# Sparse attention and a routed MLP on one core: the first five attention units in another order, one batch's values by way of DRAM, two weights loaded later

## The chip, the cores and the metric

One NeuronCore of a Trainium2 chip runs the whole program. TensorE (PE) multiplies, VectorE (DVE), ScalarE (ACT) and GpSimd (POOL) do element-wise work, and DMAs are issued from the queues of SyncE (SP), ACT and POOL. Each engine takes its instructions in the order in which the program gives them, and waits at the first one whose operands or buffers are not ready. Times are microseconds (us) on the device. The time of a kernel is the median of its runs.

## What is computed

The reference, cut to what matters (8 batches, 8 heads, 512 local and 32 global tokens, heads of 64; 8 experts, model width 512, hidden width 1024):

```python
def attention(q_l, k_l, v_l, q_g, k_g, v_g):
    scale = 1 / sqrt(64)
    v_all = concatenate([v_g, v_l], axis=2)
    # the 32 global queries see every key
    s_g = scale * q_g @ concatenate([k_g, k_l], axis=2).T
    out_g = softmax(s_g) @ v_all
    # a local query sees the global keys and the local keys at most 32 positions away
    s_ll = where(abs(i - j) <= 32, scale * q_l @ k_l.T, -1e9)
    s_l = concatenate([scale * q_l @ k_g.T, s_ll], axis=-1)
    out_l = softmax(s_l) @ v_all
    return concatenate([out_g, out_l], axis=2)

def routed_mlp(x, w_gate, w1, w2):            # x: the 4352 tokens of the attention, 512 wide
    P = exp(x @ w_gate - max)
    for _ in range(8):                        # rows, then columns, are brought to a fixed sum
        P /= P.sum(1, keepdims=True) + 1e-9
        P /= P.sum(0, keepdims=True) + 1e-9
        P *= N / E
    for e in range(8):
        out += P[:, e:e+1] * (maximum(x @ w1[e], 0) @ w2[e])
```

Inputs and the output are 32-bit floats. The kernel works in 16-bit floats with sums in 32 bits.

## The kernel before

**Units.** The local attention is cut into 32 units. Unit n is a pair of heads, hp = n mod 4, of batch n // 4. Eight blocks of 64 queries of each of the two heads lie side by side, and a block sees 128 local keys and the 32 global ones. The steps of a unit are functions, and each gives work to several engines:

- `st_A(n)`: eight transposes on PE bring the unit's keys and queries into the tile "pt". DVE copies the keys to `kTe[n % 8]`, ACT the queries to `qbd[n % 2]` (two copies).
- `st_B0(n, part)` for batch 0, `st_B(n, part)` for the others, parts 0, 1 and 2 with three, three and two blocks: the scores on PE. In batch 0 the mask is added by PE with the matrix `m16`, DVE takes the minima (the scores have their sign turned), and ACT takes the exponentials. From batch 1 on one DVE instruction adds `mask` and takes the minima, and the exponentials read its output. Batch 0 reads the global keys from `kg0T`, the others from `kgT`.
- `st_N(n, ...)`: DVE divides the exponentials by their sums in two pieces, and POOL divides the columns of the global keys ("Pl").
- `st_D1(n)`: eight transposes of the divided exponentials on PE, one copy on DVE ("pw"). `st_D2(n)`: two transposes of Pl on PE, one copy on ACT ("pg").
- `st_E(n)`: 32 matmuls with the values, and one copy of the result into `xT[batch]` (on ACT in batch 0, on DVE in batch 1). With the last unit of a batch SP stores `xT` to DRAM (`xd`).

**Values.** `st_E` needs the values of a batch in rows of 128 tokens in two alignments: `va` begins 32 tokens ahead of the first one, `vb` 32 tokens behind it. Batches 0 and 1 load them with four consecutive tokens in each partition (`load_vrow`), POOL casts them to the one tile `vsr` in two halves (`cast_vrow`), and `select_v` picks the rows for block j of `va` or `vb` by four matmuls with the 0/1 matrix `zsel` into a PSUM tile "pv", which DVE (even j) or ACT (odd j) copies. The later batches load both alignments from DRAM (`load_v`).

**Buffers.** Tiles with one tag take turns in a fixed number of buffers. PSUM has two buffers for "tr" (pt, the D1 and D2 transposes, the transposes of the global keys), two for "sc" (scores of parts 0 and 1), two for "mm" (scores of part 2 in batch 0, pv, the hidden layer's ph) and one for "po" (the result of E, one pv in each select_v that names it, and the global queries' scores). An instruction that fills a buffer waits for the last reader of what was in it.

**Global queries.** `cast_g` on POOL casts the global keys and queries, `transpose_g` on PE brings them to `kgT` and `qgT`, and `st_G0` to `st_G3` compute their attention in between.

**Hidden layer in the gaps.** From slot 4 on `f1(...)` puts single tiles of the hidden layer x @ w1[e] of experts 0 to 3 between the attention's steps: four matmuls of 512 columns on PE into "ph", then ACT ("a") or DVE ("v") takes the maximum with zero into `hT`. `f1("aa")` is two of them. They need all four heads' pairs of the batch in `xT`, and the weights `w1e[e]`, which POOL loads with a cast (`load_w1e`, 1 MB each, on POOL's DMA queue). What the attention did not take is done in the iterations over P and behind them (`tail_run`). Then the rest of the experts runs.

**Order.** Nothing reorders the program: the order of the calls is the order on each engine and in each DMA queue. Units 0 to 3 are the loop `for s in range(HP)` from L518 on: scores of unit s, D1 and D2 of unit s-1, loads and casts that depend on s, A of unit s+1, selections, divisions of unit s; E of units 0 to 2 comes in where selections allow it. From unit 4 on, the loop `for s in range(HP, NU + 1)` has a pass for each slot s: scores of unit s in three parts, D1, D2 and E of unit s-1, A of unit s+1, f1 between them, divisions at the end. The pass of slot 4 has a branch of its own, with most of batch 1's selections and the two ACT-queue copies that fill the rest of `vb` from `va`.

The helper `tt` (L672) issues most DVE operations of the second half. In the profile L346 is the division, L334 the minima, L338 and L309 the exponentials, L155 the selections, L466 the hidden layer's matmuls, L378 and L381 E.

Of the kernel before, what the change touches and what calls it, by code (L numbers as in the profile page):

```python
# [23 lines left out]
def kernel(  # L24
# [19 lines left out]
    P = 128  # L44
# [45 lines left out]
    with tc.tile_pool(name="att_c", bufs=1) as att_c, \  # L90
# [21 lines left out]
        vg16 = [dscr.tile([Sg, H, Dh], FP16, name=f"vg16_{b}") for b in range(B)]  # L112

# [29 lines left out]
        def cast_vrow(b):  # L143
            f = vraw.pop(b)
            for g in range(2):
                h = slice(4 * g, 4 * g + 4)
                nc.gpsimd.tensor_copy(out=vsr[:, :, h, :], in_=f[:, h].rearrange("p h s d -> p s h d"))

        def select_v(b, t, js, po=()):
            for j in js:  # L150
                c0 = P * j + HB * t
                pool, tag = (ps_po, "po") if j in po else (ps_mm, "mm")
                pv = pool.tile([P, D], FP32, tag=tag, name="pv")
                for so in range(NJ):
                    nc.tensor.matmul(pv, zsel[:, so, c0 : c0 + P], vsr[:, so], start=(so == 0), stop=(so == NJ - 1))  # L155
                cp = nc.vector.tensor_copy if j % 2 == 0 else nc.scalar.copy
                cp(out=vab[b % 2][t][:, j], in_=pv.rearrange("p (h d) -> p h d", h=H))

# [82 lines left out]
        nc.gpsimd.memset(m16[:, 2, 3 * W : KW], HUGE)  # L241
        init_vgz(vgz[0], nc.gpsimd)
# [275 lines left out]
        for s in range(HP):  # L518
            for part in range(3):
                st_B0(s, part)  # L520
            if s == 3:
                st_E(1)
            if s >= 1:
                st_D1(s - 1)
                st_D2(s - 1)
            if s == 0:
                cast_vrow(0)
                cast_qk(0, 1, gq)
                load_qk(1, 0, (nc.sync, nc.sync))
                load_g(k_g, kgf)  # L530
                load_w1e(0)
                nc.vector.memset(qbd[1], 0.0)
            elif s == 1:
                load_vrow(1)
                load_qk(1, 1, (nc.sync, nc.sync))
                load_vg(1)
                init_vgz(vgz[1], nc.gpsimd)
                load_vz(1)
                qgf = hpool.tile([P, H, NJ * Dh], FP32, tag="hT", name="qgf")
                load_g(q_g, qgf)  # L540
            elif s == 2:
                load_w1e(1)
                nc.gpsimd.dma_start(out=wg_sb, in_=moe_w_gate.rearrange("(dko dki) e -> dki dko e", dki=P))
                cast_qk(1, 0, gq)
                gk0 = cast_g(kgf, 0)
            for t in (kTe[s + 2],) if s < 3 else kTe[5:7]:
                nc.vector.memset(t[:, 0:W], 0.0)
                nc.vector.memset(t[:, W + Sl :], 0.0)
            st_A(s + 1)
            if s < 2:  # L550
                select_v(0, s, (0, 1), (0,))
            st_N(s, 0, 6)
            if s == 0:
                select_v(0, 0, (2, 3), (3,))
            elif s == 2:
                select_v(0, 1, (2, 3))
                st_E(0)
            st_N(s, 6, NHB)
            if s == 3:
                st_E(2)  # L560
            if s == 2:
                cast_vrow(1)
            if s == 3:
                transpose_g(gk0, 0, kgT)
                for t in qgbd:
                    nc.vector.memset(t, 0.0)
                select_v(1, 0, range(2))
                load_w1e(2)
                nc.vector.memset(mask[:, :, KW:SW], 0.0)
                nc.scalar.mul(mask[:, :, 0:KW], m16, -HUGE * 8.0)  # L570
        gat = {s: s - 5 for s in range(5, 9)}
        gat.update({2 * j + 1: j for j in range(4, NU // 2)})
        for s in range(HP, NU + 1):
# [8 lines left out]
            if s == HP:  # L582
                st_B(s, 0)
                st_D1(s - 1)
                st_D2(s - 1)
                select_v(1, 0, range(2, NJ))
                st_E(s - 1)
                select_v(1, 1, (NJ - 1,))
                slot = s + 1
                va, vb = vab[1]  # L590
                nc.scalar.dma_start(out=vb[0:HB, 0 : NJ - 1], in_=va[HB:P, 0 : NJ - 1])
                nc.scalar.dma_start(out=vb[HB:P, 0 : NJ - 1], in_=va[0:HB, 1:NJ])
                cast_qk(1, 1, gq)
            else:
                if s <= 2 * HP:
                    st_B(s, 0)
                st_D1(s - 1)
                if g23:
                    st_GN(*gp)
# [9 lines left out]
            if s < NU:  # L609
                st_B(s, 1)  # L610
            if s > HP:
                f1("va")
            if s + 1 < NU:
                st_A(s + 1)
            if s < NU:
                st_B(s, 2)
            f1("v")
            if s > HP:
                st_E(s - 1)
# [8 lines left out]
            if s < NU:  # L628
                st_N(s, 0, 6)
                st_N(s, 6, NHB)  # L630
            if s == HP:
                gcast = [(cast_g(x[0], x[1]), x) for x in ((kgf, 1, kgT), (qgf, 0, qgT), (qgf, 1, qgT))]
                load_w1e(3)
# [377 lines left out]
```

## Time and profile before

| | us |
|---|---|
| median of 3 runs | 1057.38 (1055.8 to 1061.52) |
| profiled execution | 1057.3 |
| its span, first to last instruction | 1055.5 |
| PE busy | 1025.4 |
| DVE busy | 809.6 |
| ACT busy | 489.4 |
| POOL busy | 132.2 |

"Busy" is the time in which an engine carries out instructions. Line 2 of the profile cuts the span into 40 slices of 26.4 us and gives the busy share of each in tenths; PEclk is the clock that PE was granted, as a share of its full one. Units 0 to 3 lie in the first 38 us, and unit 5's pass ends at about 61 us. A line in order of time begins with the start and the duration and ends with the idle time of the engine ahead of it and what ended that. A window's line gives each engine's busy time in it.

Some marks of the time before: the first scores of units 0 to 6 start on PE at 8.0, 14.4, 20.5, 27.4, 37.9, 47.8 and 61.3 us (of unit 6 its first part after the pass of slot 5). E(4) starts at 56.2. The weights w1e(0) to w1e(3) are issued at 13.4, 21.8, 35.2 and 52.7, the four loads of batch 2's queries and keys between 48.7 and 51.3.

### The profile page before, as it was taken

To read this page: it belongs to the slowest core of one execution; us is meant where nothing else is said; L and a number is where in the kernel's file an instruction comes from. 1 tells how busy PE (TensorE), PEld (TensorE's weight loads), DVE (VectorE), ACT (ScalarE), POOL (GpSimd) and SP (SyncE) were. 2 spreads that over 40 slices of the span, in tenths; PEclk is the share of its full clock that TensorE was granted. 3 is DMA by queue.
4 is the path that set the end of the run, shared out by engine and by line. 5 is a ranking of instruction groups with operands and counts; after the bars stand their busy time and mean duration, and the time that the engine had idled before them with its cause. 6 is when DMAs were issued, how large, how long until landed. Compare 5 with 4: busy or idle time off the path is not lost.

```text
span 1055.5 us, 21693 instructions
## 1 busy us (share of the span) xinstructions
PE 1025.4 (97%) x8854; PEld 700.0 (66%) x8854; DVE 809.6 (77%) x1466; ACT 489.4 (46%) x1248; POOL 132.2 (13%) x215
## 2 busy tenths in 40 slices
PE   7799999999999999999999999999999999999998
PEld 4455555555554466677777777777777777777787
DVE  8587777777776776997877877778777787688685
ACT  7678888787886674222222223223223233132231
POOL 7441423413313002000000000000000000000000
PEclk9899999999999999999999999999999999999999
DMA  9887598987945999935435435335336435535441
GB/s 273 200 193 211 106 261 203 218 239 156 255 130 170 270 275 303 259 106 189 170 112 194 154 140 195 125 141 199 143 117 200 168 117 177 209 100 184 170 165 31
DMA packets 97348, 190.82 MB, mean 181 GB/s; under 512 B 33425, under 2 KB 63585, under 8 KB 84449
## 3 DMA queue, kind: packets, MB, share of 16 engines
q1 hardware_dynamic: 54208, 159.61, 43.6%
q0 software_dynamic: 40432, 20.20, 14.8%
q10 hardware_dynamic: 2608, 9.64, 2.4%
q8 instruction: 69, 1.13, 0.4%
q14 instruction: 31, 0.25, 0.1%
HBM read 157.11 MB, written 53.62 MB: 200 GB/s over the span
## 4 chain that ended last, share of the span: by engine, by line
PE 79%; DVE 9%; ACT 7%; issue 3%; DMA 1%; POOL 0%; ACTq 0%; SPq 0%; DVEq 0%; POOLq 0%
PE m L795 26%; PE ph L752 21%; PE ph L466 15%; PE pm L795 10%; ACT Pu L309 3%; DVE Pu L346 3%; PE ptw L357 1%; DVE h L672 1%; ACT hT L469 1%; PE pt L273 1%; ACT qbd L283 1%; DMA h<-hd 1%; PE po L378 1%; PE sc L299 1%; DVE m L409 1%
## 5 line engine op out<-in xcount | busy, mean ns | idle before, releaser
L754 ACT ACTIVATE h<-ph 128x512 f16<-128x512 f32 (+1 forms) x288 | 164.8, 573 | 405.9 <-PE ph L752 397.1
L752 PE MATMUL ph<-xs,w1s 128*128 128x512 f16 (+1 forms) x1152 | 269.4, 367 | 2.0 <-DVE o L811 2.0
L466 PE MATMUL ph<-xT,w1e 128*128 128x512 f16 (+1 forms) x1152 | 257.2, 368 | 0.2
L795 PEld LDWEIGHTS <-h 128*128 128x128 f16 x2144 | 209.8, 98 | 44.1
L795 PE MATMUL m<-w2c,s 128*128 128x256 f16 x1620 | 199.9, 273 | 0.0
L672 DVE TENSOR_TENSOR s<-h 128x1024 f16<-128x1024 f16 (+2 forms) x140 | 122.8, 919 | 91.2 <-ACT h L754 46.8
L795 PEld LDWEIGHTS <-s 128*128 128x128 f16 x1620 | 158.5, 98 | 38.2
L466 PEld LDWEIGHTS <-w1e 128*128 128x128 f16 x1152 | 105.6, 98 | 96.6 <-issue 4.5
L752 PEld LDWEIGHTS <-w1s 128*128 128x128 f16 x1152 | 112.7, 98 | 84.8 <-issue 2.3
L672 DVE TENSOR_TENSOR h<-h,pb 128x4096 f16<-128x4096 f16 (+1 forms) x35 | 148.3, 4237 | 3.1 <-DMA h<-hd 2.9
L795 PE MATMUL m<-w2c,h 128*128 128x256 f16 x1072 | 134.2, 273 | 0.0
L469 ACT ACTIVATE hT<-ph 128x512 f16<-128x512 f32 (+1 forms) x191 | 103.8, 558 | 47.5 <-PE ph L466 46.1
L795 PE MATMUL pm<-w2c,h 128*128 128x256 f16 x1072 | 122.9, 273 | 0.0
L672 DVE TENSOR_TENSOR xs<-xg,pb 128x2048 f16<-128x2048 f16 (+1 forms) x36 | 78.0, 2168 | 46.1 <-DMA pb<-pd 40.9
L309 ACT ACTIVATE Pu<-ms,mx 128x160 f16<-128x160 f32 x224 | 93.6, 420 | 3.9 <-DVE mx L306 1.5
L471 DVE TENSOR_SCALAR hT<-ph 128x512 f16<-128x512 f32 x97 | 66.8, 689 | 31.3 <-PE ph L466 30.6
L672 DVE TENSOR_TENSOR h<-h 128x1024 f16<-128x1024 f16 (+1 forms) x140 | 86.8, 661 | 0.0
L306 DVE CUSTOM_DVE_ANT_0 ms<-sc,mask 128x160 f32<-128x160 f32 x224 | 59.9, 320 | 24.5 <-PE sc L301 22.0
L350 POOL TENSOR_TENSOR Pl<-Pu,rs 128x256 f16<-128x256 f16 x32 | 24.7, 771 | 196.7 <-DVE rs L345 131.6
L811 DVE SCALAR_TENSOR_TENSOR o<-m,o 128x512 f32<-128x512 f32 (+1 forms) x72 | 43.3, 655 | 5.2 <-ACT o L809 3.5
L346 DVE TENSOR_TENSOR Pu<-Pu,rs 128x768 f16<-128x768 f16 x64 | 45.1, 705 | 2.2
L309 ACT ACTIVATION_READ_ACCUMULATOR Pu<-ms,mx 128x1 f32 x224 | 42.4, 189 | 0.0
(157 smaller groups left out, 903.7 us busy)
## 6 DMA issues: line engine op xcount, KB each, us to landing
w1s<-w1d SPq DMA_DIRECT2D x36, 1024.0 KB
h<-hd SPq DMA_DIRECT2D x32, 1024.0 KB
hd<-hT SPq DMA_DIRECT2D x26, 1024.0 KB
pb<-pd SPq DMA_DIRECT2D x64, 256.0 KB
w2c<-in_moe_w_dram POOLq DMA_DIRECT2D x16, 512.0 KB, 21.0
out_dram<-o SPq DMA_DIRECT2D x8, 1024.0 KB
f<-in_q_l_dram SPq DMA_DIRECT2D x15, 512.0 KB
f<-in_k_l_dram SPq DMA_DIRECT2D x15, 512.0 KB
```

What stands on the lines that cost most here:

```text
L306: nc.vector.tensor_tensor_reduce(out=ms[:, ii, :], in0=sc[:, SW * ii : SW * (ii + 1)], in1=mask[:, mi, :], scale=-scale, scalar=BIG, op0=A ...
L309: nc.scalar.activation(out=d["Pu"][:, i, :], in_=ms[:, ii, :], func=AF.Exp, scale=-1.0, bias=d["mx"][:, i : i + 1], accum_out=d["sm"][:, i ...
L346: nc.vector.tensor_tensor(out=d["Pu"][:, i0:i1, 0:KW], in0=d["Pu"][:, i0:i1, 0:KW], in1=d["rs"][:, i0:i1].unsqueeze(2).to_broadcast([P, i1 ...
L350: nc.gpsimd.tensor_tensor(out=d["Pl"], in0=d["Pu"][:, :, KW:SW], in1=d["rs"].unsqueeze(2).to_broadcast([P, NHB, Sg]), op=ALU.mult)
L466: nc.tensor.matmul(ph[:, 0:n], wts[e][:, dk, P * fm : P * (fm + 1)], xT[m][:, dk, :], start=(dk == 0), stop=(dk == DP - 1))
L469: nc.scalar.activation(out=hT[:, fm, 0:n], in_=ph[:, 0:n], func=AF.Relu)
L471: nc.vector.tensor_scalar(out=hT[:, fm, 0:n], in0=ph[:, 0:n], scalar1=0.0, scalar2=None, op0=ALU.max)
L672: nc.vector.tensor_tensor(out=out, in0=in0, in1=in1, op=op)
L752: nc.tensor.matmul(ph[:, 0:n], w1s[i][:, dk, P * fm : P * (fm + 1)], xss[i][:, dk, 0:n], start=(dk == 0), stop=(dk == DP - 1))
L754: nc.scalar.activation(out=hs[i][:, fm, 0:n], in_=ph[:, 0:n], func=AF.Relu)
L795: nc.tensor.matmul(pm[:, HD * t : HD * (t + 1)], lhs[0][:, k, lhs[1] + P * t : lhs[1] + P * (t + 1)], w[:, k, q - 1, :], start=(k == 0 and ...
L811: nc.vector.scalar_tensor_tensor(out=o, in0=p, scalar=sg / float(E), in1=o, op0=ALU.mult, op1=ALU.add)
```

## The change

Units 0 to 3 are written out without a loop. In `st_BA(n)` the transposes and copies of unit n+1 (`st_A`) stand between the second and the third score part of unit n. The divisions of unit n (`divide`) come behind the scores of unit n+1, and D1 and D2 of unit n behind these; for unit 3 the divisions come ahead of unit 4's scores. The first two score parts of unit 4 move ahead of the loop, and slot 4 has an order of its own: A(5), third part of unit 4, E(3), divisions of unit 4, first part of unit 5, then loads and casts, then f1("aa"). The f1("v") of slot 4 is not called there any more, so that its tile is computed later.

Batch 1's values are no longer selected by PE. `place_v` stores `vsr` to the rows of a DRAM tile `vd`, with its first and last 32 tokens once more at the ends, and loads `va` and `vb` from it in both alignments: five DMAs on SP's queue, the two loads behind the stores that they read. The two ACT-queue copies go. The second half of the cast to `vsr` comes behind the divisions of unit 3.

`load_w1e(1)` moves from behind the scores of unit 2 to behind the divisions of unit 2, `load_w1e(2)` from ahead of slot 4 to behind unit 5's first scores, `cast_qk(1, 1)` on POOL behind the divisions of unit 4. The memset of `qbd[1]` goes from DVE to POOL, the multiplication that fills `mask` from ACT to DVE.

```diff
+        vd = dscr.tile([Sl + 2 * W, D], FP16, name="vd")
...
-        def cast_vrow(b):
-            f = vraw.pop(b)
-            for g in range(2):
+        def cast_vrow(b, gs=(0, 1)):
+            f = vraw[b]
+            for g in gs:
...
+        def place_v(b):
+            f = vsr.rearrange("p s h d -> p s (h d)")
+            nc.sync.dma_start(out=vd[W : W + Sl].rearrange("(p s) d -> p s d", s=NJ), in_=f)
+            for r in (0, W + Sl):
+                nc.sync.dma_start(out=vd[r : r + W].rearrange("(p s) d -> p s d", s=NJ), in_=f[0 : W // NJ])
+            for t, r in zip(vab[b % 2], (0, HB)):
+                nc.sync.dma_start(out=t.rearrange("p j h d -> p j (h d)"),
+                                  in_=vd[r : r + Sl].rearrange("(j p) d -> p j d", p=P))
...
+        nc.gpsimd.memset(qbd[1], 0.0)
...
-        for s in range(HP):
-            for part in range(3):
-                st_B0(s, part)
-            if s == 3:
-                st_E(1)
-            if s >= 1:
-                st_D1(s - 1)
-                st_D2(s - 1)
...
-            st_A(s + 1)
-            if s < 2:
-                select_v(0, s, (0, 1), (0,))
-            st_N(s, 0, 6)
-            if s == 0:
-                select_v(0, 0, (2, 3), (3,))
-            elif s == 2:
-                select_v(0, 1, (2, 3))
-                st_E(0)
-            st_N(s, 6, NHB)
...
-                select_v(1, 0, range(2))
-                load_w1e(2)
-                nc.vector.memset(mask[:, :, KW:SW], 0.0)
-                nc.scalar.mul(mask[:, :, 0:KW], m16, -HUGE * 8.0)
+        def st_BA(n):
+            st_B0(n, 0)
+            st_B0(n, 1)
+            pad_k((kTe[n + 1],))
+            st_A(n + 1)
+            st_B0(n, 2)
+
+        def divide(n):
+            st_N(n, 0, 6)
+            st_N(n, 6, NHB)
+
+        cast_vrow(0)
+        cast_qk(0, 1, gq)
+        st_BA(0)
+        load_qk(1, 0, (nc.sync, nc.sync))
+        load_g(k_g, kgf)
+        load_w1e(0)
+        select_v(0, 0, (0, 1), (0,))
+        st_BA(1)
+        divide(0)
+        select_v(0, 0, (2, 3), (3,))
+        st_D1(0)
+        st_D2(0)
+        load_vrow(1)
+        load_qk(1, 1, (nc.sync, nc.sync))
+        load_vg(1)
+        init_vgz(vgz[1], nc.gpsimd)
+        load_vz(1)
+        qgf = hpool.tile([P, H, NJ * Dh], FP32, tag="hT", name="qgf")
+        load_g(q_g, qgf)
+        select_v(0, 1, (0, 1), (0,))
+        st_BA(2)
+        divide(1)
+        st_D1(1)
+        st_D2(1)
+        nc.gpsimd.dma_start(out=wg_sb, in_=moe_w_gate.rearrange("(dko dki) e -> dki dko e", dki=P))
+        cast_qk(1, 0, gq)
+        gk0 = cast_g(kgf, 0)
+        select_v(0, 1, (2, 3))
+        st_B0(3, 0)
+        st_B0(3, 1)
+        st_E(0)
+        pad_k(kTe[4:7])
+        st_A(4)
+        st_B0(3, 2)
+        divide(2)
+        load_w1e(1)
+        cast_vrow(1, (0,))
+        nc.vector.memset(mask[:, :, KW:SW], 0.0)
+        nc.vector.tensor_scalar(out=mask[:, :, 0:KW], in0=m16, scalar1=-HUGE * 8.0, scalar2=None, op0=ALU.mult)
+        st_E(1)
+        st_D1(2)
+        st_D2(2)
+        transpose_g(gk0, 0, kgT)
+        divide(3)
+        cast_vrow(1, (1,))
+        place_v(1)
+        st_B(4, 0)
+        st_E(2)
+        for t in qgbd:
+            nc.vector.memset(t, 0.0)
+        st_D1(3)
+        st_B(4, 1)
+        st_D2(3)
...
             if s == HP:
-                st_B(s, 0)
-                st_D1(s - 1)
-                st_D2(s - 1)
-                select_v(1, 0, range(2, NJ))
+                st_A(s + 1)
+                st_B(s, 2)
                 st_E(s - 1)
-                select_v(1, 1, (NJ - 1,))
+                st_N(s, 0, 6)
+                st_N(s, 6, NHB)
+                st_B(s + 1, 0)
                 slot = s + 1
-                va, vb = vab[1]
-                nc.scalar.dma_start(out=vb[0:HB, 0 : NJ - 1], in_=va[HB:P, 0 : NJ - 1])
-                nc.scalar.dma_start(out=vb[HB:P, 0 : NJ - 1], in_=va[0:HB, 1:NJ])
+                load_w1e(2)
                 cast_qk(1, 1, gq)
+                gcast = [(cast_g(x[0], x[1]), x) for x in ((kgf, 1, kgT), (qgf, 0, qgT), (qgf, 1, qgT))]
+                load_w1e(3)
```

The conditions in the rest of the loop only leave out, in slots 4 and 5, what these lines already do. `gcast` and `load_w1e(3)` stood at the end of slot 4, behind the divisions of unit 4, and are still behind these.

More of the change, by code (lines that the diff above doesn't have):

```diff
@@ L517, with pad_k @@
         cast_first(1, 1, nc.vector.tensor_copy)
-        for s in range(HP):
-            for part in range(3):
-                st_B0(s, part)
-            if s == 3:
-                st_E(1)
-            if s >= 1:
-                st_D1(s - 1)
-                st_D2(s - 1)
-            if s == 0:
[L527 to L540, printed above, removed]
-            elif s == 2:
[L542 to L546, printed above, removed]
+        def pad_k(ts):
+            for t in ts:
@@ L547 @@
                 nc.vector.memset(t[:, 0:W], 0.0)
                 nc.vector.memset(t[:, W + Sl :], 0.0)
-            st_A(s + 1)
-            if s < 2:
-                select_v(0, s, (0, 1), (0,))
-            st_N(s, 0, 6)
-            if s == 0:
-                select_v(0, 0, (2, 3), (3,))
-            elif s == 2:
-                select_v(0, 1, (2, 3))
-                st_E(0)
-            st_N(s, 6, NHB)
[L559 to L566, printed above, removed]
-                select_v(1, 0, range(2))
-                load_w1e(2)
-                nc.vector.memset(mask[:, :, KW:SW], 0.0)
-                nc.scalar.mul(mask[:, :, 0:KW], m16, -HUGE * 8.0)
+        def st_BA(n):
[7 more added lines that the diff above has]
+            st_N(n, 6, NHB)
@@ L582 @@
             if s == HP:
-                st_B(s, 0)
-                st_D1(s - 1)
-                st_D2(s - 1)
-                select_v(1, 0, range(2, NJ))
+                st_A(s + 1)
+                st_B(s, 2)
                 st_E(s - 1)
-                select_v(1, 1, (NJ - 1,))
+                st_N(s, 0, 6)
+                st_N(s, 6, NHB)
+                st_B(s + 1, 0)
                 slot = s + 1
-                va, vb = vab[1]
-                nc.scalar.dma_start(out=vb[0:HB, 0 : NJ - 1], in_=va[HB:P, 0 : NJ - 1])
-                nc.scalar.dma_start(out=vb[HB:P, 0 : NJ - 1], in_=va[0:HB, 1:NJ])
+                load_w1e(2)
                 cast_qk(1, 1, gq)
+                gcast = [(cast_g(x[0], x[1]), x) for x in ((kgf, 1, kgT), (qgf, 0, qgT), (qgf, 1, qgT))]
+                load_w1e(3)
             else:
-                if s <= 2 * HP:
+                if HP + 1 < s <= 2 * HP:
                     st_B(s, 0)
@@ L608 @@
                 st_G2(*gp)
-            if s < NU:
+            if HP < s < NU:
                 st_B(s, 1)
@@ L612 @@
                 f1("va")
-            if s + 1 < NU:
+            if HP < s < NU - 1:
                 st_A(s + 1)
-            if s < NU:
+            if HP < s < NU:
                 st_B(s, 2)
-            f1("v")
             if s > HP:
+                f1("v")
                 st_E(s - 1)
@@ L627 @@
                 f1("va")
-            if s < NU:
+            if HP < s < NU:
                 st_N(s, 0, 6)
                 st_N(s, 6, NHB)
-            if s == HP:
-                gcast = [(cast_g(x[0], x[1]), x) for x in ((kgf, 1, kgT), (qgf, 0, qgT), (qgf, 1, qgT))]
-                load_w1e(3)
             if s > 2 * HP and not g1:
```

## The prediction

> **What bounds the kernel now.** I read the page first (slices, engines), then the windows at the clock's steps, then the engines' instructions in order of time up to 62 us, and last the DMA queues by stage.
>
> ```profile
> span 1055.5 us, 21693 instructions
> PE 1025.4 (97%) x8854; PEld 700.0 (66%) x8854; DVE 809.6 (77%) x1466; ACT 489.4 (46%) x1248; POOL 132.2 (13%) x215
> ...
> PE   7799999999999999999999999999999999999998
> ...
> PEclk9899999999999999999999999999999999999999
> ```
>
> PE carries the span; only the first two slices (52 us) have gaps. Whatever is saved there reaches the end, because all later work queues on PE; whatever PE work is only moved does not.
>
> ```profile
> 21.30:24.70 3.40, 2.10 (x32) 1.63 (x30) 2.75 (x8) 2.63 (x15) 3.40 (x5) 1.00 1.14 285
> 31.50:34.90 3.40, 1.43 (x41) 1.13 (x41) 2.96 (x8) 2.72 (x7) 1.30 (x2) 1.00 1.00 192
> 34.95:38.30 3.35, 3.35 (x14) 1.43 (x13) 0.80 (x2) 0.19 (x1) 2.70 (x4) 0.50 0.79 176
> 45.20:48.50 3.30, 1.51 (x16) 0.64 (x13) 3.23 (x12) 3.26 (x13) 0.00 (x0) 1.00 0.51 106
> 48.65:51.90 3.25, 3.11 (x14) 1.49 (x13) 1.93 (x9) 1.68 (x8) 2.87 (x4) 0.50 0.88 263
> ```
>
> Columns: stretch, then busy us of PE, weight load, DVE, ACT, POOL, the granted clock, DMA share, GB/s. After 1.43 and 1.51 us of PE work the next 3.4 us ran at 0.50; after 2.10 us they did not.
>
> ```profile
> 33.60 1.04 POOL L147 CAST vsr<-vraw 128x1024 f16<-128x1024 f32 x1 [4.73 <-DVE Pu L346]
> ...
> 34.69 3.38 PE L155 MATMUL pv<-vsr,zsel 128*128 128x512 f16 x8 [1.03 <-POOL vsr L147]
> ...
> 47.75 0.23 PE L299 MATMUL sc<-kTe,qbd 128*128 128x128 f16 x1 [1.45 <-ACT qbd L283]
> ...
> 49.62 3.06 PE L466 MATMUL ph<-xT,w1e 128*128 128x512 f16 x8
> ```
>
> POOL's cast of batch 1's values stood 4.73 us, PE waited for it and did the selections at half clock; later scores of unit 5 waited for ACT. The name behind the 4.73 us was busy all the time; w1e(1) was loading (row 28 to 31 below), so I take the load of vraw for the cause.
>
> ```profile
> q0 software_dynamic: 229, 0.47, 82.4%
> q1 hardware_dynamic: 224, 0.23, 27.6%
> ...
> q1 hardware_dynamic: 1056, 1.05, 100.0%
> ```
>
> Packets, MB and share by queue; q0 is POOL's (weights), q1 SP's. From 28 to 31 us (first two lines) both moved the same number of packets, and q1 got 0.23 MB in 3 us. From 52 to 55 us (last line) q1 alone moved 1.05 MB.
>
> **The change, part by part.** The profiled execution took 1057.3 us (span 1055.5 and 1.8 around it); the median is 1057.38, 0.1 above. Durations: a unit's eight exponentials 2.98 us on ACT, its two qbd copies 1.24, a value copy 0.59 ACT or 0.61 DVE, pg 0.27; on DVE three minima 1.53, divisions 1.62, pw and kTe 0.61 each; on PE scores 1.12, transposes of A 0.45, one selection (four matmuls) 0.87, D1 0.46, E 0.55. A group of PE to its reader takes 0.62 to 0.66 (selection 1.06), minima to exponential 0.75.
>
> Step 1, units 0 and 1. A(n+1) now stands between score parts; divide(n) follows scores n+1. ACT runs unbroken from 9.48: six exponentials, qbd(1) to 12.95, two more to 13.7, value copy to 14.3; unit 1's scores leave PE from 13.0 (qbd(1)), its minima start at 13.6, its exponentials run from 14.4 to 18.6 with qbd(2) inside; value copy to 19.2. Before, ACT idled 0.84 and 0.99 for minima that stood behind the divisions on DVE; these idles go, and DVE's divisions run beside ACT. The qbd memset moved to POOL costs it about 0.95 (half of vgz's 1.87): vsr is ready at 11.05 instead of 10.3, just as score part 2 leaves PE. Covered by those score parts; without them PE's selections, and with them all behind, start 0.7 later.
>
> Step 2, a new wait. The first selection for vb uses the one "po" buffer, whose copy is that at 19.2 on ACT behind unit 1's exponentials; before it lay ahead of them. Queued behind it on PE: the second selection and unit 2's scores. 19.25 + 2 x 0.87 gives scores at 21.0; before 20.52. So 0.5 late: the copy has taken the place of the minima. Bounds: were the copy ready when PE comes to it (18.2, after D2(0)), scores would start at 19.95, 0.6 early; were PE at half clock there, 1.7 later than I say.
>
> Step 3, unit 3. PE then has 1.4 us of work to 24.7 (rest of the scores, A(3)), like the stretches that led to 0.50; I take half clock to 28.1. D1, D2 and the selections of vb follow divide(1) at 25.45; at half clock the first takes 1.74: the second runs at full clock again, and the scores of unit 3 start at 28.9 against 27.37, 1.5 late (0.6 at full clock). Its exponentials: minima 0.6, exponential 0.75 behind, 30.25 (28.74 before).
>
> Step 4, the turn to batch 1. No selections for it: 20 matmuls (4.35 us at full clock), three ACT and two DVE copies and two DMAs on ACT's queue go. Unit 4's first scores need qbd(4) and kgT. On ACT: six exponentials to 32.5, E(0)'s copy 0.6, qbd(4) to 34.3. On DVE: minima to 32.1, divide(2) to 33.7, the mask (0.14 and an estimate of 0.45, between nothing, in DVE's wait for D1(2), and the 0.69 of a kTe copy), pw at 34.4 to 35.0, the transposes for kgT, its copy to 36.4. Scores at 36.5 against 37.86. Parts 1 and 2 follow without the 2.2 and 0.87 us of selections and without the 3.8 us that ACT waited: exponentials of unit 4 end at 43.9 (before 48.66), unit 5's first scores at 43.1 (47.75), 4.6 early.
>
> Step 5, to E(4). f1 ("aa") waits for xT(3), now behind unit 4's exponentials on ACT: 44.5 (42.5 before). Two ph of 0.87 to 45.7, where before three had been done by 46.3; D1(4) to 46.15 (48.52 before, held to 49.6 by divisions that now end at 44.6). The next two ph need the buffers that ACT's hT copies free, behind the exponentials of unit 5 (45.1 to 46.35): 47.0 to 48.7. B(5,1) at 48.85 (52.63); from there two ph, A(6), part 2 and one ph as before, 3.65, lead to E(4): 52.5 against 56.17. Gain 3.7.
>
> Step 6, moved fill. One f1 ("v") leaves slot 4; its 0.87 us of PE return before the end (there PE releases every hT copy). Minus 0.87.
>
> Step 7, clock. About 1.5 us of PE work from 38.3 to 41.8 again: half clock may follow, costing 0 to 0.9 (one ph doubled); 0.4 taken. Before paid 1.1 at 49.6 (two ph 2.85 instead of 1.74), which is in step 5's gain. The Trainium skill, "TensorE: Matmul & The Clock Gate", section "What's actually happening", has the array return to half clock after about 3.4 us of idle window; the trace agrees in length (34.9 to 38.3, 48.55 to 51.95) but throttled after windows 40% busy. By that rule my stretches, none of them idle, would not throttle: gain 3.7 instead of 2.4.
>
> Step 8, POOL and SP. Weights: w1e(1) is issued at 34 instead of 21.8 and needed by the ninth f1 near 53; landings took 10.3 to 13.2, so covered by some 6 us. w1e(2) at 45, needed at slot 7. POOL has cast_qk(1,1) behind Pl(4) (about 44.3) and w1e(2): 48, needed by A(6) near 51; the three gcasts (3.05) to 51, needed at 53: covered. SP: place_v waits for the second cast (39.6), the stores' landing, then issues two reads; behind them xd and the four loads of batch 2 (issued 48.7 to 51.3 before) wait, needed at 62; covered. Stores: first packet 0.8 after issue (xd: 48.2 to 49.0), 1.5 to 3 for 0.58 MB, to be seen 0.2 to 1.4 later (vb<-va, pd): landed 43.3 to 45.5. Reads of 1 MB in 1 KB rows: 3 us at q1's free rate, 13.6 beside weights at 75 packets per us: values at 48.5 to 60. I take 49 to 52, because w1e(3), issued at 52.69 into a full q1, put its first packet there at 56.2: E(4) at 52.5 just isn't held.
>
> Sum: 3.7 - 0.87 - 0.4 = 2.4 us: 1057.3 - 2.4 = 1054.9, against the median 1055.0.
>
> **Rivals.** (a) Values late, the other side. If w1e(2) and w1e(3) reach the DMA engines first, 1024 packets at 75 per us from 45.5 take until 59.1, landed at 60; E(4), and all of PE behind it, stands 7.5 us. 60 - 56.17 + 0.87 = 4.7, and a half-clock stretch after the stall (1.7): 1063.7. It decides once vb lands after 55.3, 2.8 behind E(4). For it: 28 to 31 us; against: 52 to 56 us. The Trainium skill, "DMA: Bandwidth & Descriptors", section "Queues, rings and completion order", says that each DMA engine takes its queues in turn, packet by packet; the equal packets from 28 to 31 us agree, the 52 to 56 us do not. (b) PE keeps its clock: 0.9 from step 3 and 0.4 from step 7 more, 3.7, 1053.6; with step 2's lower bound (1.1 more) 4.8: 1052.5, and the sum of all such bounds is near 5.8. For: 2.10 us was enough; against: I count 1.4. (c) The early units lose more: each half-clock stretch doubles two selections (1.74) or E and D1 (1.0), and ACT, in order, repeats the delay: 2.4 gone, 1057.3. (d) The loads later free nothing: the 4.73 us was DVE's doing and POOL stands again before place_v; values 3 us later, 1058.
>
> **How the numbers follow.** Sum as worked out 0.40 (own range 1053 to 1057), (b) 0.24, (c) 0.12, (d) 0.08, (a) 0.16. What a measurement tells from no change is about 0.5%, 5.3 us: below 1052.1 or above 1062.7. Faster: most of (b) and a little of the first, 0.20. Slower: most of (a), 0.14. Within: 0.66. Range 1051.0 to 1062.0, which leaves out half of (a) and a tail of (b).
>
> **What would show it.** Unit 2's scores at 21.0 waiting for an ACT va copy; clock 0.50 somewhere between 24 and 39; unit 4's scores near 36.5, unit 5's near 43; E(4) near 52.5 without a wait named for a DMA; last landing of w1e after 60. Wrong if PE stands over 2 us before E(4), if POOL's casts wait for f, or if unit 2's scores come before 20.

## The result: 0.4% slower, and the wait that did it

The changed kernel takes 1062.03 us in the median (1061.25 to 1064.47, 10 runs) against 1058.36 for the kernel before (1055.8 to 1061.52, 10 runs beside it): ratio 1.0038, 95% interval 1.0028 to 1.0049. The forecast was 1055.0 and its range ended at 1062.0. The values came late, as rival (a) had it.

The profiled execution after took 1062.15 us. First its page, the span, the engines, and the slices of PE and its clock:

```profile
span 1060.4 us, 21663 instructions
...
PE 1025.6 (97%) x8834; PEld 700.5 (66%) x8834; DVE 807.5 (76%) x1465; ACT 487.6 (46%) x1245; POOL 132.3 (12%) x216
...
PE   6879999999999999999999999999999999999998
...
PEclk9789999999999999999999999999999999999999
```

PE's busy time is as before (1025.4), and the 20 matmuls of the selections are gone from the count; the loss is a hole in the third slice (53.0 to 79.5 us, 9 before), with a lower clock in it. Next PE's instructions in order of time, in the changed kernel (start, duration, what; in brackets the idle time ahead and what ended it):

```profile
19.13 1.89 PE L156 MATMUL pv<-vsr,zsel 128*128 128x512 f16 x8 [0.85 <-ACT va L158]
...
26.05 3.45 PE L156 MATMUL pv<-vsr,zsel 128*128 128x512 f16 x8
...
36.78 0.18 PE L312 MATMUL sc<-kgT,qbd 128*128 128x32 f16 x1 [0.62 <-DVE kgT L219]
...
43.56 3.21 PE L477 MATMUL ph<-xT,w1e 128*128 128x512 f16 x8
...
58.56 0.27 PE L389 MATMUL po<-pw,vb 128*64 128x64 f16 x2 [5.88 <-DMA vb<-vd]
```

PE has come to E(4) at 52.43, does its first two matmuls with `va` and two with the global values, and stands 5.88 us for `vb`. In the kernel before E(4) had no wait:

```profile
56.17 0.22 PE L378 MATMUL po<-pw,va 128*64 128x64 f16 x2
```

The chain of waits of the changed kernel, in order of time, goes from the store to the read to PE:

```profile
39.84 5.36 DMA vd<-vsr
...
45.75 12.77 DMA vb<-vd
...
58.56 0.27 PE po L389 x2
```

The stores took 5.4 us to be seen as landed, the read of `vb` 12.8. The queues of the changed kernel, first from 38 to 41 us, then from 49 to 50, then from 50 to 54 (packets, MB, share of 16 engines; q0 carries POOL's weights, q1 SP's stores and reads):

```profile
q0 software_dynamic: 308, 0.63, 112.1%
```

```profile
q0 software_dynamic: 99, 0.20, 108.0%
```

```profile
q0 software_dynamic: 306, 0.63, 84.8%
q1 hardware_dynamic: 290, 0.30, 27.0%
```

In the first stretch w1e(1) has the DMA engines to itself; the stores, issued at 39.84, put their first packet there at 41.8, as w1e(1) ends. In the second w1e(2), whose first packet came at 48.4, has them to itself, and the reads, about half done by then, move nothing. In the third the reads go packet for packet with w1e(2), whose packets are twice as large. The clock by stretch in the changed kernel (busy us of PE, weight load, DVE, ACT, POOL; granted clock; DMA share; GB/s):

```profile
22.50:25.90 3.40, 0.88 (x11) 0.49 (x10) 2.95 (x10) 3.36 (x15) 0.94 (x2) 0.98 1.16 310
25.90:29.10 3.20, 3.20 (x10) 1.27 (x11) 1.20 (x2) 0.88 (x5) 3.20 (x4) 0.50 1.09 317
...
36.50:46.30 9.80, 8.67 (x110) 6.26 (x110) 7.64 (x35) 7.16 (x28) 3.68 (x6) 0.50 0.73 167
53.20:56.60 3.40, 0.00 (x0) 0.00 (x0) 0.09 (x1) 1.14 (x5) 0.00 (x0) 0.99 1.08 243
56.60:66.80 10.20, 7.82 (x91) 4.86 (x92) 5.33 (x11) 0.60 (x1) 2.24 (x6) 0.50 1.09 293
```

From 56.5, still in the stall, the clock is at half for 10.2 us. Unit 6's first scores come at 66.19 against 61.33 before: 4.86 late, and the span is 4.9 longer. So between the two profiled executions the whole loss is made ahead of unit 6. (The medians lie 3.7 apart; the profiled execution of the kernel before ran 1.1 below its median.)

### The profile page after: what moved, and what is told of

It reads as the page before. It is cut to its first block, busy times and chain, and to the rows that moved or that the text cites. A ratio compares the mean times of both kernels' runs of the same rounds, so it can differ in the third digit from the quotient of the medians.

```text
span 1060.4 us, 21663 instructions
## 1 busy us (share of the span) xinstructions
PE 1025.6 (97%) x8834; PEld 700.5 (66%) x8834; DVE 807.5 (76%) x1465; ACT 487.6 (46%) x1245; POOL 132.3 (12%) x216
## 4 chain that ended last, share of the span: by engine, by line
PE 78%; DVE 8%; ACT 7%; issue 3%; DMA 3%; POOL 1%; SPq 0%; ACTq 0%; DVEq 0%; POOLq 0%
PE m L819 26%; PE ph L776 21%; PE ph L477 14%; PE pm L819 10%; ACT Pu L320 3%; DVE Pu L357 2%; PE ptw L368 1%; DVE h L696 1%; DMA vb<-vd 1%; ACT hT L480 1%; ACT qbd L294 1%; DMA h<-hd 1%; PE po L389 1%; PE pt L284 1%; DVE m L420 1%
## 5 line engine op out<-in xcount | busy, mean ns | idle before, releaser
L480 ACT ACTIVATE hT<-ph 128x512 f16<-128x512 f32 (+1 forms) x192 | 104.4, 558 | 55.1 <-PE ph L477 42.9
L317 DVE CUSTOM_DVE_ANT_0 ms<-sc,mask 128x160 f32<-128x160 f32 x224 | 59.9, 319 | 17.8 <-PE sc L312 17.3
```

What stands on the lines that cost most here:

```text
L317: nc.vector.tensor_tensor_reduce(out=ms[:, ii, :], in0=sc[:, SW * ii : SW * (ii + 1)], in1=mask[:, mi, :], scale=-scale, scalar=BIG, op0=A ...
L480: nc.scalar.activation(out=hT[:, fm, 0:n], in_=ph[:, 0:n], func=AF.Relu)
```

## The experiments

All ratios are to the kernel before, run on the same chip, where it took 1058.25 to 1058.40. The ratio and its interval are as recorded; the quotient of the two medians differs from the ratio by up to 0.001. The theory after the result (A): `vb` is late because weight loads have the DMA engines, first ahead of the stores, then beside the reads. Rivals: the loads of batch 2 on SP's own queue are to blame (R); the rows by DRAM are slow in themselves; the new order of the units costs.

### What holds the values: three loads moved in the changed kernel

w1e(2) and w1e(3) behind the reads:

```diff
-                load_w1e(2)
                 cast_qk(1, 1, gq)
                 gcast = [...]
-                load_w1e(3)
...
                 st_G0(*gn)            # in the pass of slot 5
+                load_w1e(2)
+                load_w1e(3)
```

> The changed kernel with w1e(2) and w1e(3) issued by POOL behind the global queries' copies of slot 5, so behind E(4), and nothing else. Theory A (the two weights' packets hold the reads of va and vb): the stores land near 45 as before, both reads land by 50, PE comes to E(4) near 52.4 and is not held (5.9 us go), the clock stays full from 52 on (half clock from 56.6 to 66.9 goes, 2.5 us between E(4) and unit 6's first scores). Together 8.5 us less than the changed kernel: about 1053.5, 0.45% below the kernel before. Rival R (the way through memory is too long by itself, or SP's own queue holds it: stores, their landing, reads, and the loads of batch 2 behind them): vb still lands after 55, and the time stays within 2 us of 1062.

1053.89 us, ratio 0.9967 (0.9951 to 0.9984). From the chain of this run, and from PE's order of time:

```profile
38.77 6.76 DMA vd<-vsr
...
46.03 5.48 DMA vb<-vd
```

```profile
51.55 0.22 PE L389 MATMUL po<-pw,vb 128*64 128x64 f16 x2 [0.49 <-DMA vb<-vd]
```

The read takes 5.5 us instead of 12.8 and the hold shrinks from 5.88 to 0.49: two DMAs that were moved bring 8.1 us of the median. So the way by DRAM isn't too slow in itself. The stores still take 6.8: most of w1e(1)'s packets run until 40.5, and the last of qgf's loads lie ahead of the stores on their own queue.

SP's own loads of batch 2 moved in the program instead:

```diff
-                    load_qk(b + 1, 0, (nc.sync, nc.sync))
-                    load_qk(b + 1, 1, (nc.sync, nc.sync))
+                    if s > HP:                      # batch 2's go behind st_G0 of slot 5
+                        load_qk(b + 1, 0, (nc.sync, nc.sync))
+                        load_qk(b + 1, 1, (nc.sync, nc.sync))
```

> The changed kernel with the four loads of batch 2's queries and keys issued by SP behind E(4) instead of right behind the two reads. Theory A: the weights still share the DMA engines packet by packet with the reads, E(4) is held 4 us or more, time 1060 to 1063. Rival R (SP's own queue): the reads land by 51, E(4) is not held, about 1053.5.

1062.85 us, ratio 1.0039 (1.0023 to 1.0055), and still, in the chain of this run:

```profile
45.76 12.99 DMA vb<-vd
```

But this run does not test R. Between the two places in the program SP has nothing else to issue, so it issued the first of the four at 46.80 in the changed kernel and at 46.80 here:

```profile
46.80 0.60 SPq L121 DMA_DIRECT2D f<-in_q_l_dram  x1
```

The run before this one settles R: there, too, the four loads follow right behind the reads, and the read took 5.5 us all the same:

```profile
47.08 0.43 SPq L121 DMA_DIRECT2D f<-in_q_l_dram  x1
```

R falls by that. Only w1e(1) moved, ahead of the stores, the other two left in the way:

```diff
         gk0 = cast_g(kgf, 0)
+        load_w1e(1)
...
         divide(2)
-        load_w1e(1)
```

> The changed kernel with w1e(1) alone issued earlier (about 29.6 instead of 33.1 to 34.7); w1e(2) and w1e(3) stay ahead of the reads at 45 and 51. Theory A (the values are late by two holds, the stores behind w1e(1) and the reads beside w1e(2) and w1e(3)): stores landed at 42 to 43.5, reads issued by 44, their packets ahead of most of w1e(2)'s (first packet 3.4 us behind its issue): vb landed at 48 to 53, E(4) held 0 to 1 us: 1053 to 1055.5, ratio 0.995 to 0.998. Theory B (w1e(2) and w1e(3) hold the reads wherever these are): vb landed after 55.5, E(4) held over 3 us, 1059.5 to 1062.

1054.91 us, ratio 0.9972 (0.9956 to 0.9988). SP's issues and then PE in this run:

```profile
39.68 0.35 SPq L162 DMA_DIRECT2D vd<-vsr  x1
...
43.34 0.38 SPq L166 DMA_DIRECT2D va<-vd  x1
```

```profile
51.94 0.22 PE L389 MATMUL po<-pw,vb 128*64 128x64 f16 x2 [0.77 <-DMA vb<-vd]
```

The reads are issued 1.9 us earlier than in the changed kernel (45.27), and w1e(2)'s first packet comes 3.9 us behind them (47.3) instead of 3.2 (48.4). In that 0.7 us the reads go alone, at some 380 packets per us (188 and 187 in half a microsecond each in the changed kernel); beside w1e(2) they go at 72 (290 in 4 us). So 0.7 us of lead is, by my estimate, some 270 packets or 3.7 us of sharing. `vb` comes 6.6 us earlier (51.94 for 58.56). The 1.9, the 3.7 and the microsecond in which the reads of the changed kernel moved nothing (49 to 50; there is no such stretch here) add up to that. The hold shrinks by less, 5.1, because PE, at full clock around 26 us in this execution, also comes to E(4) 1.5 us earlier. Both together:

```diff
# w1e(1) behind gk0, w1e(2) and w1e(3) behind st_G0 of slot 5
```

> The run with w1e(2) and w1e(3) behind slot 5's casts, and w1e(1) besides issued behind the first cast of the global rows (about 29.6) instead of 33.1, so that its packets are through before the stores are issued at 38.4. Theory A (a weight load in flight holds the stores): first packets of the stores within 1.5 us of their issue, landed 42 to 43.5 instead of 45.5, vb landed by 49.5, E(4) without the wait of 0.5 us: 1052.5 to 1054, ratio to the kernel before 0.994 to 0.9965. Theory B (the 6.8 us from issue to landing are the stores' own): landed at 45 as before, the same time as the run it is made from. If w1e(1) delays the load of batch 1's rows instead, the first cast waits on POOL and the time is up to 1 us longer.

1053.47 us, ratio 0.9957 (0.9943 to 0.9972). E(4) starts at 50.83 without a wait for a DMA; the reads were issued at 43.48. The time is in A's range, 0.4 below the run with w1e(1) in its place, which is within the intervals.

### What each part is worth without the hold

The last run looked like the gain that the prediction put on the new order. Four runs take the parts one by one. The new order with PE's selections, weights where the change has them:

```diff
-        place_v(1)
...
         st_E(2)
+        select_v(1, 0, range(2))
...
         st_B(s, 2)
+        select_v(1, 0, range(2, NJ))
         st_E(s - 1)
+        select_v(1, 1, (NJ - 1,))
+        va, vb = vab[1]                 # and the two copies on ACT's queue
```

> The changed kernel with PE's selections for batch 1 (20 matmuls, five copies) and the two DMAs on ACT's queue back in place of the way through memory; the order of the units and the later weights as changed. E(4) is not held in any theory. If the new order itself gains (unit 4's and 5's scores early, as the trace of the changed kernel shows), the time is e1's plus the part of 4.35 us of selections that doesn't fit in PE's gaps between 39 and 46 us (2 to 4 us): 1055.5 to 1057.5, at or a little below the kernel before. Rival (the gain came from leaving out the selections alone): 1058 or more.

1059.33 us, ratio 1.0007 (0.9994 to 1.002): a miss of my range, and inside the rival's (1058 or more). The order alone gains nothing. With the weights clear as well:

```diff
# as above, w1e(1) behind gk0, w1e(2) and w1e(3) behind st_G0 of slot 5
```

> The changed kernel's order of the units with batch 1's selections by PE and the two copies on ACT's queue, w1e(1) behind the first cast of the global rows, w1e(2) and w1e(3) behind slot 5's casts. With the run that has rows in the same order (1053.5) and the two in the old order it tells what each of order and rows brings when no weight load is in the way. Theory A (order worth nothing, rows worth nothing): 1053 to 1054.5, ratio 0.995 to 0.9965. Theory B (in this order the selections' 4.35 us are on the path and the rows take them off it): 1055.5 to 1058, ratio 0.9975 to 1.0.

1059.3 us, ratio 1.0019 (1.0006 to 1.0032). Theory B of this run, and a little beyond it. PE's order of time:

```profile
39.96 3.57 PE L156 MATMUL pv<-vsr,zsel 128*128 128x512 f16 x8 [1.63 <-POOL vsr L148]
```

The second cast of the rows comes behind unit 3's divisions in this order, and PE waits for it and does the selections at half clock. That wait is the one that the prediction saw in the kernel before, made by the order instead of by a load.

The other way round, the rows in the old order, weights as in the kernel before:

```diff
                 cast_vrow(1)
+                place_v(1)
...
-                select_v(1, 0, range(2))        # and the other selections and ACT's two copies
```

> The kernel before with one part of the change alone: batch 1's values by way of rows in memory, place_v right behind the cast; order and weights as before. Theory A: the stores (issued near 35) wait for w1e(2), which has the DMA engines from 36.8 to 43, and land near 45; the reads then find the DMA engines free until w1e(3) at 56 and land by 50; E(4), which PE reaches near 51.5 without the selections, is held 1 us at most: 4 to 6 us less than before, 1052.5 to 1054.5. Rival R (the way through memory is too long): E(4) held past 55, within 2 us of the kernel before.

1056.83 us, ratio 0.9991 (0.9979 to 1.0003): a miss too. E(4) is held past 55 and the time is within 2 us of the kernel before, as R had it, but the way by DRAM is not slow in itself (5.5 us for the read above). POOL, SP and PE in this run:

```profile
35.17 1.04 POOL L148 CAST vsr<-vraw 128x1024 f16<-128x1024 f32 x1 [5.35 <-DMA vraw<-in_v_l_dram]
```

```profile
40.67 0.36 SPq L162 DMA_DIRECT2D vd<-vsr  x1
...
50.18 0.38 SPq L166 DMA_DIRECT2D va<-vd  x1
```

```profile
54.10 0.27 PE L388 MATMUL po<-pw,va 128*64 128x64 f16 x2 [2.33 <-DMA va<-vd]
...
55.85 0.26 PE L388 MATMUL po<-pw,vb 128*64 128x64 f16 x2 [1.42 <-DMA vb<-vd]
```

The reads go out 9.5 us behind the store here, with w1e(2) (issued at 36.7) in the engines until 46 and qgf's loads ahead of the store on SP's queue, and E(4) is held again. The first line speaks for a name: the wait of POOL for 4.73 us in the kernel before, which the profile put down to DVE, is named a DMA of `vraw` here, where w1e(1) stands as before. A run below, with w1e(1) alone moved, shows it.

So the weights later alone, in the old order with selections:

```diff
-                load_w1e(1)                      # slot 2, ahead of the casts
...
                 cast_vrow(1)
+                load_w1e(1)
...
-                load_w1e(2)                      # ahead of slot 4
...
+                load_w1e(2)
                 load_w1e(3)
```

> The kernel before with one part of the change alone: w1e(1) issued behind the second cast of batch 1's rows, w1e(2) just ahead of w1e(3); the order of the units and the selections by PE stay. Theory A (weights in flight while something waits for its data is what costs): the second cast of the rows on POOL no longer waits 4.7 us for its load, but the selections behind it are held by unit 4's scores and divisions anyway; w1e(2) and w1e(3) go out together at about 52, past the two copies of vb on ACT's queue: nothing gained or lost, 1057 to 1059.5. Theory B (the 4.7 us of POOL set the turn to batch 1 in the kernel before): E(4) comes 1 to 3 us earlier and the time is 1055 to 1057.

1053.49 us, ratio 0.996 (0.9947 to 0.9973). I had expected nothing from it, and it is faster than both theories allowed. And of these moves only the first:

```diff
-                load_w1e(1)
...
                 cast_vrow(1)
+                load_w1e(1)
```

> The kernel before with one load moved: w1e(1) issued behind the second cast of batch 1's rows (about 29.7) instead of ahead of the first (21.8). Theory A (w1e(1) in flight delays the rows' own load by 4.7 us, and that delay, with the selections at half clock behind it, sets E(4) in the kernel before): no wait of POOL for vraw, the selections start near 33.3 and take 1.9 us instead of 3.4, E(4) near 52 instead of 56: 1053 to 1055, ratio 0.995 to 0.997, as in the run with all three weights later. Theory B (w1e(2), issued at 39 beside vb's two copies, is the load that costs): nothing or less than 1 us gained, 1057 to 1059.

1053.40 us, ratio 0.9962 (0.9947 to 0.9976): one DMA issue moved by 9 us (21.8 to 31.0) is worth 4.9 us of the median. In its profile, PE and then POOL:

```profile
33.41 1.90 PE L155 MATMUL pv<-vsr,zsel 128*128 128x512 f16 x8
...
46.85 1.89 PE L466 MATMUL ph<-xT,w1e 128*128 128x512 f16 x8
...
52.24 0.22 PE L378 MATMUL po<-pw,va 128*64 128x64 f16 x2
```

```profile
29.98 1.04 POOL L147 CAST vsr<-vraw 128x1024 f16<-128x1024 f32 x1 [0.74 <-DMA vraw<-in_v_l_dram]
```

Against the lines of before: POOL's two casts of the rows wait 0.7 us each instead of 4.73 for the first, the selections start 1.3 earlier and take 1.90 instead of 3.38, and the eight matmuls at 46.85 take 1.89 instead of 3.06. PE is granted its full clock from 20 to 60 us, and E(4) starts at 52.24, 3.9 earlier. The earlier start (1.3) and the two groups of matmuls that the kernel before did at half clock (2.7) add up to that.

The clock has a large part in this gain. The 82 executions of the kernel before that ran beside the experiments differ by their mean granted clock: 41 of them had 0.995 and took 1057.5 to 1059.8 us, two had 1.000 and took 1053.4 and 1053.7. That is as fast as this run, whose twelve executions had 0.998 or 1.000. What the wait for the rows costs without the half clock behind it, no run separates.

The rows in the old order with every load out of their way (the selections and ACT's two copies go here too):

```diff
-                load_g(q_g, qgf)
...
                 cast_vrow(1)
+                place_v(1)
+                load_g(q_g, qgf)
...
-                load_w1e(2)
+                load_w1e(1)           # behind unit 3's divisions; w1e(2), w1e(3) in slot 5
```

> The kernel before with the values of batch 1 by way of rows and nothing in their way: place_v right behind the casts of the rows, the loads of qgf behind it on SP's queue, w1e(1) behind the divisions of unit 3, w1e(2) and w1e(3) behind slot 5's casts; no selections for batch 1; the order of the units as before. Theory A (the 20 matmuls of the selections, 4.35 us, lie on the path to E(4) once the loads are clear): vb landed by 44, E(4) at 48 to 50.5 (52.1 with selections and later weights): 1050 to 1052.5, ratio 0.992 to 0.9945. Theory B (ACT's and DVE's exponentials and divisions set the turn to batch 1, the selections only fill PE's idle time): E(4) at 51 to 52.5, 1053 to 1054.5, ratio 0.995 to 0.9965.

1052.29 us, ratio 0.9953 (0.9937 to 0.9969). The time lies in theory A's range and the ratio in theory B's, so it decides neither. The four cases with the weights out of the way:

| | selections by PE | rows by DRAM |
|---|---|---|
| old order | 1053.49, 1053.40 | 1052.29 |
| new order | 1059.30 | 1053.47 |

Rows are worth 5.8 us in the new order, where the cast comes late, and 1.2 in the old one; the new order costs 5.8 with selections and 1.2 with rows. The 5.8 are far outside the intervals. The 1.2 are within them, though six of the eight executions with rows in the old order (1050.3 to 1052.6) lie below the fastest of the twelve with w1e(1) moved alone (1053.06), so a small gain is likely.

### The half clock

Fillers in the changed order, all weights clear (reading constants, written to a PSUM tile that nobody reads):

```diff
+        def filler(n):
+            pf = ps_mm.tile([P, 512], FP32, tag="mm", name="pf")
+            for _ in range(n):
+                nc.tensor.matmul(pf[:, 0 : 3 * KW], bigI, m16.rearrange("p a c -> p (a c)"), start=True, stop=True)
...
         st_BA(2)
+        filler(11)
...
         st_B0(3, 2)
+        filler(8)
...
+        filler(3)
         transpose_g(gk0, 0, kgT)
```

> The run with all three weights clear of the stores and reads, and 22 matmuls of 128x384 added that write a spare PSUM tile nothing reads: 11 behind the scores of unit 2, 8 behind the scores of unit 3, 3 ahead of the transposes for kgT, all where PE stood idle (2.3, 1.8 and 0.6 us). Theory C (the lower granted clock from 35 to 45, in steps 3 and 7 of the prediction, costs PE time on the path): the granted clock stays 1.00 or is lower for less than half as long, the first eight matmuls of f1 take 1.74 to 1.9 us instead of 3.0, E(4) comes 1.0 to 1.8 us earlier and the time is 1 to 2 us below the run without them. Theory D (ACT and DVE are the path there, PE's clock costs nothing): the same time within 0.5 us, E(4) where it was. If the fillers push the scores, transposes or selections, up to 1 us longer.

1053.57 us, ratio 0.9958 (0.9943 to 0.9973): no gain over the 1053.47 without them, as theory D had it. The profiled execution was late by 4 us before the first filler, with its clock at 0.50 from 22.5 to 25.5 and again from 46.5 to 49.5. In the stretch that was meant its clock was full (1.00 from 26 to 46 us), where the run without fillers had 0.50 from 33.8 to 44.0, and yet from E(1) to E(4) it took 19.3 us against 18.9. The same in the old order with rows:

```diff
# filler(6) ahead of st_E(2), filler(3) behind transpose_g, filler(3) behind st_D1(3)
```

> The run with rows and clear weights in the old order, and 12 matmuls of 128x384 added that write a spare PSUM tile nothing reads: 6 ahead of E(2), where PE stood 1.2 us, 3 behind the transposes for kgT (0.5 us), 3 behind the transposes of unit 3 (0.6 us). There the granted clock fell to 0.50 from 36 to 42.7, which it did not in the old order with selections. Theory C (the selections taken away leave PE too little work, and the half clock that follows, not the path, eats part of the gain): granted clock 1.00 from 30 to 60, the first eight matmuls of f1 take 1.9 us instead of 3.0, 0.7 to 1.5 us gained: 1050.8 to 1051.8, ratio 0.993 to 0.995. Theory D (ACT and DVE set that stretch and the clock costs nothing): the same time as without the fillers within 0.5 us, 1052 to 1052.8.

1052.10 us, ratio 0.9946 (0.9927 to 0.9965), theory D's range again. Windows without the fillers and with them; the profiled execution without them came to unit 2 some 2 us late, so its windows are put later:

```profile
32.20:35.60 3.40, 1.58 (x45) 1.35 (x45) 2.73 (x10) 3.38 (x14) 0.17 (x1) 1.00 0.54 174
35.85:42.60 6.75, 5.37 (x55) 3.32 (x55) 2.52 (x11) 3.58 (x11) 3.14 (x4) 0.51 0.92 233
```

```profile
31.50:34.90 3.40, 3.01 (x61) 2.20 (x60) 3.02 (x10) 2.92 (x8) 1.87 (x3) 1.00 0.54 181
34.90:38.30 3.40, 2.43 (x44) 1.45 (x42) 1.26 (x7) 2.18 (x8) 1.70 (x2) 1.00 0.92 145
```

PE's busy time in the window rises from 1.58 to 3.01 us, the clock stays at 1.00, and from E(2) to E(4) it is 17.5 us instead of 19.0 in the profiled executions. The medians differ by 0.2, within what either is known by. That work for nothing kept the clock is seen in these profiled executions, one of each kernel; that it makes the kernel faster is not shown. This speaks against a large price of the half clock, the 82 executions of the kernel before speak for one, and what it costs stays open. This version has the lowest median of all (6.3 us under the kernel before).

## Why the prediction was wrong, step by step

Step 8 failed: "I take 49 to 52" for the landing of the values. Measured 58.5, near the upper bound of 60. One of its terms was small: "first packet 0.8 after issue" for the stores was 2.0, behind w1e(1), which that step costed only for its own due time (with nothing in flight, in the run with rows in the old order and every load out of their way, 0.8 holds: 32.19 to 33.0); the landing, 45.2, still fell in the range given. The other decided: "w1e(3) ... put its first packet there at 56.2" (56.4 by the packets of that trace) was read as a load that gives way to a full q1. It does not give way once its packets flow. In the changed kernel w1e(2) is issued at 45.1 and its first packet comes at 48.4; then it has the engines alone, and from 50 on it shares them one to one. Nor does the delay ahead of the first packet follow q1: in the run with w1e(1) and w1e(2) later in the old order, w1e(2) went out at 49.8 into a full q1 (some 360 packets per us) and put its first packet there 1.5 us later, while w1e(2) of the changed kernel took 3.3 although the engines moved next to nothing from 43.5 to 46 (12 packets). What sets the delay stays open.

So rival (a) was given 0.16 on the strength of a row that showed a delay of the load, not a priority. Its mechanism was in the main as written, except that the reads reached the engines first, by some 2 us: 75 packets per us foreseen and 72 measured, landing at 60 foreseen and 58.5 measured, PE standing 7.5 foreseen and 5.9 measured, half clock with it, 1063.7 foreseen and 1062.0 measured. The rule named there (the Trainium skill, "DMA: Bandwidth & Descriptors", section "Queues, rings and completion order", queues in turn packet by packet) agrees with 50 to 54 us, 306 packets to 290. It doesn't describe 49 to 50, where w1e(2) moved 99 packets and the reads none, nor, if the stores' 0.8 holds beside a load, 40.6 to 41.8, where w1e(1) kept its rate of 50 packets per half a microsecond and the stores had none.

Steps 1 and 2 were right: vb's selections wait for ACT's copy of `va` (19.13), unit 2's scores at 20.86 (21.0 foreseen). Step 3 was right for this execution (unit 3's scores at 29.34 against 28.9), but by chance: with the same work up to there, the runs with weights behind, with all clear and with w1e(1) earlier kept the full clock and came to E(1) 1.5 us earlier; the other runs of this order without fillers fell to half like the changed kernel. Steps 4 and 5 were right in size: unit 4's scores wait for kgT until 36.78 (36.5; one matmul that needs no kgT goes at 35.94), unit 5's come at 43.14 (43.1), E(4) is reached at 52.43 (52.5).

But a term of the sum was put on the wrong part. Those 3.7 us were credited to the new order and to the selections that go. The kernel with w1e(1) moved and nothing else has E(4) at 52.24. In the sum, w1e(1)'s move stood only as something to be "covered"; I had read its effect on POOL (4.73 us) as the cause of the late selections in the first view, and did not ask what the old order would do without it. Rival (d), that the loads later free nothing, is refuted by that run, in which POOL's wait fell to 0.7.

Step 6 (0.87 of fill moved) fits: with all clear E(4) is 1.4 earlier than in the old order with w1e(1) moved, and the times are equal. No run measured it alone. Step 7 was mis-sized: half clock from 36.0 to 46.3 instead of one window, and eight matmuls at 43.56 in 3.21 us instead of 1.89, 1.3 against 0.4. What that costs at the end stays open.

The rule of the Trainium skill weighed in step 7 ("TensorE: Matmul & The Clock Gate", section "What's actually happening": half clock after an idle window of about 3.4 us) asks for too much here again: the clock fell at 36.0 after 1.9 us of work in 3.4 (32.6 to 36.0), and at 56.5 after none (53.1 to 56.5), which alone is the rule's case. The same section says that the window runs freely and does not start with the kernel; that agrees with step 3's two outcomes, 0.88 us of work in the same 3.4 us, followed by 0.50 here and, with weights behind, by

```profile
22.50:25.90 3.40, 0.88 (x12) 0.46 (x9) 2.95 (x10) 3.36 (x15) 0.91 (x2) 1.00 1.15 303
26.00:29.20 3.20, 3.20 (x60) 2.19 (x59) 1.98 (x4) 1.51 (x7) 3.20 (x4) 1.00 0.99 279
```

## What to carry to other kernels

A transfer that something waits for has to be priced against every load in flight from its issue to its landing; in this kernel its packets went one to one with the load's at best, and for a stretch not at all. A bulk load that nobody needs soon goes behind it. Before a gain is put on a reordering, ask what the smallest edit in the change would give by itself: here one DMA issued 9 us later gave all that the sum had put on the path to E(4), and the rest of the change added a new wait for the same DMA engines. A delay between issue and first packet is not evidence of priority. An issue that is moved in the program moves in time only if its queue has something between the two places; look at the issue times before a run is called a test.

## What the runs showed of the hardware that was not expected

- A store to DRAM and the read of it are short only when nothing else is in flight. From the store's issue to that of the reads it took 3.2 us with nothing else in flight (rows in the old order, all clear), 3.7 and 5.1 in the two runs with w1e(1) early, where SP's own smaller loads were still in flight, 5.4 in the changed kernel, 7.2 with w1e(2) and w1e(3) behind, and 9.5 beside w1e(2) with qgf's loads ahead.
- How a load on POOL's queue and transfers on SP's share the engines differs within one kernel: one to one from 50 to 54 us, the load alone from 49 to 50, and alone, while the stores were due, from 40.6 to 41.8. What decides between the two was not tried.
- The half clock lasts for about 3.4 us or a multiple: 3.4, 10.2 and 10.2 us in the changed kernel, 6.8 in the run with rows in the old order and all clear. In the changed kernel it went on after stretches of 3.4 us with 1.4 to 3.0 us of PE work (36.0 to 39.4: 2.8; 59.9 to 63.3: 3.0) and ended after those with 3.3 to 3.4 (25.8 to 29.2, 42.9 to 46.3, 63.3 to 66.8).
